# A seventeenth score tile per head group for VectorE, and a quarter of most images for GpSimd, in a one-core attention and spectral kernel

## The chip, the cores and the metric

One core of a Trainium2 chip. Its engines run side by side, each through its own list of instructions in order: TensorE (PE: matmuls, results in the banks of PSUM), ScalarE (ACT), VectorE (DVE), GpSimd (POOL, which works on SBUF here) and SyncE (SP, which issues DMAs). They wait for each other through semaphores. The metric is the device time of one execution in microseconds; lower is better.

## The reference, cut to what matters

```python
x = A_x                                       # 1 x 2048 x 512, bf16
x = x + _A_ref(_layernorm(x), A_w_r, A_w_i)   # irfft2(rfft2(x) * (w_r + i w_i))
x = x + _B_ref(_layernorm(x), wq, wk, wv, wo) # attention
x = x + _A_ref(_layernorm(x), A_w_r, A_w_i)
x = x + _B_ref(_layernorm(x), wq, wk, wv, wo)

def _B_ref(x, wq, wk, wv, wo):                # 32 heads of 16; one k and one v for all heads
    q = (x @ wq).reshape(B, S, 32, 16).transpose(0, 2, 1, 3)
    k = x @ wk
    v = x @ wv
    p = softmax(einsum("bhqd,bkd->bhqk", q, k) * 16 ** -0.5)
    return einsum("bhqk,bkd->bhqd", p, v).transpose(0, 2, 1, 3).reshape(B, S, 512) @ wo
```

Nearly all of the time goes into the exponentials of the two attention layers: 32 x 2048 x 2048 of them in each.

## The kernel before, in words

An attention layer works through 32 **groups** (`NG`): 4 blocks of 512 queries, each with 8 groups of 4 heads. The 2048 keys are cut into 16 chunks `kc` of 128, so a group has 64 **score tiles** (128 keys x 512 queries, one of 16 chunks and 4 heads). A score tile is one matmul with 32 rows of contraction (`score`, line 601), and its exponentials then go into a matmul with the values (`pv_step`, line 713) that adds up in one PSUM bank `pv` for the whole group. The values carry a column of ones, so that the sum of the exponentials comes out in the same bank.

Two engines make the exponentials, in two ways:

- **ScalarE** takes 48 of the 64 tiles, three at a time: `act_step(n)` writes three score tiles into the three banks of a PSUM tile `sc` (two buffers) and takes one `Exp` over all 1536 columns into `e` (line 701).
- **VectorE** takes the other 16, those with `h == kc % 4`. For each, `dve_step(n)` has a score matmul written into the one PSUM bank `dv` (one buffer) and turns it into 16-bit integers, a scaled logarithm: the **conversion** `t_new <- dv` (line 725). Four of them, of four neighbouring chunks, make a batch `b` of 4 x 512 integers. From each batch VectorE makes four **images** (lines 729 to 732): half the integers plus one of four offsets `PH_OFF`, whose bits are then read as bf16. The four images, each multiplied with values of its own weight (`vaug[:, j]`), add up to the exponential. So every VectorE tile needs four value matmuls, a ScalarE tile one.

The order is written out by hand. The layer is a run of **steps** `n`, one for each `e`; a group has 16 of them (the first group 18). In a step come, in this order, work put off by earlier steps (`todo`), the eviction of the group before, `dve_step`, `act_step`, `pv_step`. `chain()` ties each engine's instructions into exactly this order. In every step of a steady group VectorE does one conversion and one image, 16 and 16 per group. Value matmuls come two steps after their exponentials (`LAG = 2`).

The change of group lies in the third and fourth step of the next group:

```python
o, den = evict(evict_at[n])          # step 2: o <- pv, PSUM to SBUF, VectorE (line 616)
...
qproj(qproj_at[n], ps)               # step 2: queries of a later group, four matmuls into the freed pv bank
later(1, lambda ...: QT.__setitem__(g, qevict(ps)))   # step 3: qt <- ps and a bitwise and, VectorE (lines 464, 465)
```

In step 6 VectorE takes the reciprocal of the sums (line 624), which SP's DMAs bring and spread again. From step 12 on GpSimd multiplies `o` with them in three cuts (`product`, line 657). `pace` (line 605) makes such a GpSimd instruction wait for the latest image that VectorE has been given, so that it begins when that image has ended.

Around the two attention layers lie the spectral layers (Fourier transforms as matmuls), whose work the change does not touch. Their tile `U` (tag `G` of the pool `shared`) is free while attention runs.

Of the kernel before, what the change touches and what calls it, by code (L numbers as in the profile page):

```python
# [10 lines left out]
ALU = mybir.AluOpType  # L11
P = 128
BF = mybir.dt.bfloat16
F32 = mybir.dt.float32
I32 = mybir.dt.int32
S, D, H, DH = 2048, 512, 32, 16
NF = D // 2 + 1
NT = 16
NC = 4
R = 4  # L20
T = 4
# [5 lines left out]
I16 = mybir.dt.int16  # L27
# [15 lines left out]
def host_tables():  # L43
    import ml_dtypes
    bf = lambda a: np.ascontiguousarray(np.asarray(a, dtype=np.float32).astype(ml_dtypes.bfloat16))
    f32 = lambda a: np.ascontiguousarray(np.asarray(a, dtype=np.float32))
    w0 = 2 * np.pi / 2048.0
    tabs = {}

    sp = (128 * np.arange(4)[None, None, :, None] + np.arange(P)[:, None, None, None]).astype(np.float64)  # L50
    tt = np.arange(4)[None, :, None, None].astype(np.float64)
    k1 = np.arange(256)[None, None, None, :].astype(np.float64)
    ang = w0 * k1 * (4 * sp + tt)
    alt = np.broadcast_to(1.0 - 2.0 * (sp % 2), ang.shape[:3] + (1,))
    tabs["FT"] = bf(np.concatenate([np.cos(ang), -np.sin(ang)[..., 1:], alt], axis=3))

    s1 = np.arange(512)[None, None, None, :].astype(np.float64)
    kk = (128 * np.arange(2)[None, None, :, None] + np.arange(P)[:, None, None, None]).astype(np.float64)
    angi = w0 * kk * (4 * s1 + tt)
    wgt = np.where(kk == 0, 0.5, 1.0)  # L60
    it = np.stack([wgt * np.cos(angi), -np.sin(angi)], axis=2)
    it[0, :, 1, 0, :] = 1.0 - 2.0 * (np.arange(512) % 2)
    tabs["IT"] = bf(it)

    dd = (128 * np.arange(4)[None, :, None] + np.arange(P)[:, None, None]).astype(np.float64)
    ff = (np.arange(256)[None, None, :] + 1).astype(np.float64)
    angd = 2 * np.pi * dd * ff / 512.0
    tabs["DT"] = bf(np.stack([np.cos(angd), np.sin(angd), -np.sin(angd), 2 * np.sin(angd), -2 * np.sin(angd)], axis=2))
    fr = (128 * np.arange(2)[None, :, None] + np.arange(P)[:, None, None] + 1).astype(np.float64)
    d1 = np.arange(512)[None, None, :].astype(np.float64)  # L70
    angp = 2 * np.pi * fr * d1 / 512.0
    cfac = np.where(fr == 256, 1.0, 2.0) / (S * D)
    tabs["PS"] = bf(np.stack([cfac * np.cos(angp), cfac * np.sin(angp), -cfac * np.sin(angp)], axis=2))

    col = np.arange(64)
    c_, k2_, q_ = col // 32, (col // 8) % 4, col % 8
    base = 32 * k2_ + 8 * c_ + q_
    sel = np.zeros((P, 5, 64))
    sel[base, 0, col] = 1.0
    sel[(128 - base) % 128, 1, col] = 1.0  # L80
    sel[127 - base, 2, col] = 1.0
    sel[:, 3:5] = -sel[:, 1:3]
    tabs["SEL"] = bf(sel)
    selx = np.zeros((P, 2, 4))
    for i, (p_, sg) in enumerate(((16, 1), (48, 1), (112, -1), (80, -1))):
        selx[p_, 0, i] = 1.0
        selx[p_, 1, i] = sg
    tabs["SELX"] = bf(selx)
    eye = np.eye(P, dtype=np.float32)
    half = (np.arange(P) % 32) // 16  # L90
    tabs["KAB"] = f32(np.stack([1.0 - half, -THETA * half], axis=1))
    tabs["QAND"] = np.ascontiguousarray(np.broadcast_to(np.where(half == 0, -1, 0x7FFF).astype(np.int16)[:, None], (P, 512)))
    tabs["ident"] = bf(eye)
    return tabs

# [350 lines left out]
def attention_inputs(nc, tabs, shared, xn_sb, aw):  # L446
# [15 lines left out]
    def qevict(ps):  # L462
        qt = shared.tile([P, 512], BF, tag="QT", bufs=3)
        nc.vector.tensor_copy(out=qt, in_=ps)  # L464
        nc.vector.tensor_tensor(out=qt.bitcast(I16), in0=qt.bitcast(I16), in1=tabs["QAND"], op=ALU.bitwise_and)  # L465
        return qt

    def filler(psum, rhs, n):
# [60 lines left out]
def attention_layer(nc, tc, tabs, shared, lnpool, x_sb, xn_sb, aw, prep, nxt, store):  # L529
    with ExitStack() as ctx:  # L530
# [24 lines left out]
        NG = NQB * HG  # L555
        s0 = {}
        act_tiles = []
        for g in range(NG):
            s0[g] = len(act_tiles)
            us = [(g, kc, h) for kc in range(NT) for h in range(4)  # L560
                  if h != kc % 4 or (g == 0 and kc < 4)]
            act_tiles += [us[i:i + 3] for i in range(0, len(us), 3)]
        s0[NG] = len(act_tiles)
        d_score, d_phase = {}, {}
        for g in range(NG):
            for kc in range(NT):
                if not (g == 0 and kc < 4):
                    d_score[s0[g] + kc - 4] = (g, kc)
                    if g == 0:
                        base = 4 + (kc // 4 - 1) * 4  # L570
                    else:
                        base = s0[g] + kc - kc % 4
                    d_phase[base + kc % 4] = (g, kc // 4, kc % 4)
        LAG = 2
        first_pv, last_pv = {}, {}
        pv_list = {}
        evict_at = {s0[g + 1] + LAG: g for g in range(NG)}
        qproj_at = {s0[g + 1] + LAG: g + 2 for g in range(NG - 2)}
        for n0 in range(s0[NG]):
            lst = []  # L580
            if n0 in d_phase:
                g, b, j = d_phase[n0]
                lst += [(g, 4 * b + i, i, j, n0) for i in range(4)]
            lst += [(g, kc, h, -1, n0) for (g, kc, h) in act_tiles[n0]]
            assert len({u[0] for u in lst}) == 1
            n = n0 + LAG
            if n in evict_at:
                n += 1
            pv_list.setdefault(n, []).extend(lst)
            for u in lst:  # L590
                first_pv.setdefault((u[0], u[2]), u)
                last_pv[(u[0], u[2])] = u

        psc = ctx.enter_context(tc.tile_pool(name="psc", bufs=2, space=bass.MemoryType.PSUM))
        psd = ctx.enter_context(tc.tile_pool(name="psd", bufs=1, space=bass.MemoryType.PSUM))
# [3 lines left out]
        def score(dst, g, kc, h):  # L599
            hs = slice(32 * h, 32 * h + 32)  # L600
            nc.tensor.matmul(dst, lhsT=KT[hs, kc * P:(kc + 1) * P], rhs=QT[g][hs, :], start=True, stop=True)  # L601
# [3 lines left out]
        def pace(ins):  # L605
            if image[0] is not None:
                tc.add_manual_dep(ins.ins, image[0].ins.name, mybir.DependencyInfo(
                    mybir.DependencyClass.Sync, mybir.DependencyReason.DATA), reason="pace")
# [80 lines left out]
                store(r, t, nc.sync if t == T - 1 and r % 2 == 1 else nc.gpsimd)  # L689

        chain()
        def act_step(n):
            if n >= s0[NG]:
                return
            sc = psc.tile([P, 3, 512], F32, tag="sc")
            for i, (g, kc, h) in enumerate(act_tiles[n]):
                score(sc[:, i, :], g, kc, h)
            na = len(act_tiles[n])
            e = work.tile([P, 3, 512], BF, tag="e", bufs=7)
            ex[n] = e  # L700
            nc.scalar.activation(out=e[:, 0:na, :], in_=sc[:, 0:na, :], func=ACT.Exp, scale=SCALE)  # L701

        def pv_step(n):
            for u in pv_list.get(n, ()):
                g, kc, h, j, n0 = u
                if g not in pv:
                    pv_new = psp.tile([P, 512], F32, tag="pv")
                    pv[g] = pv_new
                if j < 0:
                    rhs = ex[n0][:, act_tiles[n0].index((g, kc, h)), :]  # L710
                else:
                    rhs = sb[(g, kc // 4, j)][:, h, :].bitcast(BF)
                nc.tensor.matmul(pv[g][32 * h:32 * h + 32, :], lhsT=vaug[:, max(j, 0), kc, :], rhs=rhs,  # L713
                                 start=(g > 0 and first_pv[(g, h)] == u), stop=(last_pv[(g, h)] == u),
                                 skip_group_check=True)

        def dve_step(n):
            if n in d_score:
                g, kc = d_score[n]
                dv = psd.tile([P, 512], F32, tag="dv")  # L720
                score(dv, g, kc, kc % 4)
                if kc % 4 == 0:
                    t_new = work.tile([P, 4, 512], I16, tag="T", bufs=3)
                    tb[(g, kc // 4)] = t_new
                nc.vector.tensor_scalar(out=tb[(g, kc // 4)][:, kc % 4, :], in0=dv, scalar1=T_MUL, scalar2=T_ADD,  # L725
                                        op0=ALU.mult, op1=ALU.add)
            if n in d_phase:
                g, b, j = d_phase[n]
                s_new = work.tile([P, 4, 512], I16, tag="S", bufs=7)
                sb[(g, b, j)] = s_new  # L730
                image[0] = nc.vector.tensor_scalar(out=s_new, in0=tb[(g, b)], scalar1=0.5, scalar2=16384.0 + PH_OFF[j],  # L731
                                                   op0=ALU.mult, op1=ALU.add)

        for n in range(s0[NG]):
            now[0] = n
# [281 lines left out]
```

## Time and profile before

| | us |
|---|---|
| median of 3 runs | 1649.36 (1648.85 to 1650.64) |
| the profiled execution's own time | 1655.24 |
| span in its profile, first to last instruction | 1653.4 |
| PE, DVE, ACT, POOL busy | 1428.4, 1551.4, 1509.0, 163.2 |
| ACT, all `e` (1028) | 1387.5 |
| DVE, conversions (1016) and images (1016) | 695.5 and 698.6 |
| POOL, `product` in three cuts (186) | 104.4 |

A "busy" time is the union of the instructions' spans. VectorE's instructions overlap their neighbours: the next one is shown to start about 85 ns before the last one ends, so a mean of 0.69 us for a conversion stands for some 0.60 us of the engine's time. The profiled execution is 0.36% longer than the median of the runs; differences that are worked out from its rows are added to the median as they are. From the eviction of one group to that of the next the trace shows 21.6 us all through both attention layers.

### The profile page before, as it was taken

The numbers are of one execution on the slowest core, as the hardware profiler recorded it, in microseconds if no ns is written. First come the engines' busy times: TensorE is split into PE (matmuls) and PEld (weight loads), VectorE is DVE, ScalarE is ACT, GpSimd is POOL, SyncE is SP. The second block draws the span as 40 slices with busy tenths as digits, with TensorE's granted clock in tenths as the row PEclk, the third lists the DMA queues.
The fourth block names the chain that finished last, engine by engine and source line by source line (L and its number), as shares of the span: only waits on it lengthen the run. The fifth ranks groups of instructions, "written<-read, shape, count | busy, mean of one in ns | idle before, by whom it ended". The sixth has DMA issues, their size and how long they took to land.

```text
span 1653.4 us, 32260 instructions
## 1 busy us (share of the span) xinstructions
PE 1428.4 (86%) x12768; PEld 461.3 (28%) x12768; DVE 1551.4 (94%) x2793; ACT 1509.0 (91%) x1254; POOL 163.2 (10%) x277
## 2 busy tenths in 40 slices
PE   6798888888888888888988988888888888888887
PEld 2342222222222222222333322222222222222222
DVE  6979999999999999999778799999999999999995
ACT  5369999999999999999853799999999999999994
POOL 3210000000000000000102000000000000000002
PEclk9899999999999999999998999999999999999999
DMA  8000000000000010001020000000000000000002
GB/s 289 5 1 8 17 17 17 17 16 11 16 17 17 16 30 16 16 17 30 23 71 0 1 9 16 17 17 17 17 17 17 17 17 17 12 15 17 16 17 66
DMA packets 46536, 40.78 MB, mean 25 GB/s; under 512 B 30832, under 2 KB 34416, under 8 KB 46000
## 3 DMA queue, kind: packets, MB, share of 16 engines
q1 hardware_dynamic: 45712, 36.88, 7.9%
q8 instruction: 100, 1.64, 0.4%
q0 software_dynamic: 672, 1.84, 0.3%
q14 instruction: 52, 0.43, 0.1%
HBM read 33.57 MB, written 3.15 MB: 22 GB/s over the span
## 4 chain that ended last, share of the span: by engine, by line
ACT 32%; DVE 29%; issue 21%; PE 16%; POOL 1%; DMA 1%; SPq 0%; DVEq 0%; POOLq 0%; ACTq 0%
ACT e L701 31%; DVE t_new L725 11%; DVE s_new L731 9%; PE pv_new L713 4%; PE fd L268 2%; PE dv L601 2%; DVE o L616 2%; DVE qt L464 2%; PE sc L601 2%; DVE qt L465 1%; DVE stats L125 1%; PE tri L679 1%; PE ps L391 1%; PE ps L379 1%; PE ps L192 1%
## 5 line engine op out<-in xcount | busy, mean ns | idle before, releaser
L701 ACT ACTIVATE e<-sc 128x1536 bf16<-128x1536 f32 (+1 forms) x1028 | 1387.5, 1532 | 6.2 <-PE sc L601 5.8
L725 DVE TENSOR_SCALAR t_new<-dv 128x512 int16<-128x512 f32 x1016 | 695.5, 685 | 26.4 <-PE dv L601 8.9
L731 DVE TENSOR_SCALAR s_new<-t_new 128x2048 int16<-128x2048 int16 x1016 | 698.6, 689 | 0.0
L601 PE MATMUL dv<-qt,KT 32*128 32x512 bf16 x1016 | 384.1, 378 | 108.1 <-DVE t_new L725 106.0
L601 PE MATMUL sc<-qt,KT 32*128 32x512 bf16 x3080 | 409.0, 383 | 33.9 <-ACT e L701 4.3
L713 PE MATMUL pv_new<-s_new,vaug 128*32 128x512 bf16 x4064 | 410.4, 391 | 27.2 <-DVE qt L464 27.2
L713 PE MATMUL pv_new<-e,vaug 128*32 128x512 bf16 x3080 | 412.9, 390 | 0.3 <-ACT e L701 0.3
L601 PEld LDWEIGHTS <-KT 32*128 32x128 bf16 x4096 | 201.2, 91 | 721.4 <-issue 702.8
L713 PEld LDWEIGHTS <-vaug 128*32 128x32 bf16 x7144 | 135.3, 94 | 265.7 <-issue 251.2
L657 POOL TENSOR_TENSOR ot_new<-o,rb 128x176 bf16<-128x176 f32 (+1 forms) x96 | 55.0, 575 | 700.0 <-DVE s_new L731 649.3
L657 POOL TENSOR_TENSOR od<-o,rb 128x176 bf16<-128x176 f32 (+1 forms) x90 | 49.4, 549 | 598.7 <-DVE s_new L731 598.7
L459 PE MATMUL ps<-xT,wq_sb 128*128 128x512 bf16 x256 | 67.3, 387 | 11.4 <-DVE o L616 11.4
L379 PE MATMUL ps<-tab_PS,st 128*128 128x512 bf16 x128 | 36.1, 448 | 16.2 <-DVE st L327 12.7
L385 ACT CAST U<-ps 128x512 bf16<-128x512 f32 x24 | 14.0, 585 | 36.4 <-PE ps L379 36.4
L268 PE MATMUL fd<-X,tab_DT 128*128 128x512 bf16 x192 | 43.9, 390 | 2.7 <-DVE X L242 2.7
L274 ACT CAST xn_sb<-fd 128x512 bf16<-128x512 f32 x32 | 18.7, 585 | 28.5 <-PE fd L268 28.5
L464 DVE CAST qt<-ps 128x512 bf16<-128x512 f32 x64 | 44.2, 691 | 0.4 <-PE ps L459 0.4
L616 DVE COPY o<-pv_new 128x512 f32<-128x512 f32 x64 | 43.8, 685 | 0.2 <-PE dv L601 0.2
L125 DVE BATCH_NORM_STATS2 stats<-x_sb 128x6 f32<-128x512 bf16 x46 | 30.7, 676 | 7.2 <-DMA x_sb<-in_A_x_dram 3.5
L459 PEld LDWEIGHTS <-wq_sb 128*128 128x128 bf16 x256 | 25.0, 97 | 40.2 <-issue 16.6
L391 PE MATMUL ps<-U,IT 128*128 128x512 bf16 x128 | 34.3, 390 | 0.0
L192 PE MATMUL ps<-FT,xn_sb 128*128 128x512 bf16 x80 | 22.2, 439 | 13.9 <-ACT xn_sb L134 10.9
(154 smaller groups left out, 602.1 us busy)
## 6 DMA issues: line engine op xcount, KB each, us to landing
rb<-d SPq DMA_DIRECT2D x256, 64.0 KB
FT<-const_FT SPq DMA_DIRECT2D x8, 512.0 KB
IT<-const_IT SPq DMA_DIRECT2D x8, 512.0 KB
x_sb<-in_A_x_dram SPq DMA_DIRECT2D x4, 512.0 KB
ot_new<-od SPq DMA_DIRECT2D x120, 16.0 KB
out_dram<-x_sb POOLq DMA_DIRECT2D x14, 128.0 KB, 2.2
tab_DT<-const_DT SPq DMA_DIRECT2D x1, 1280.0 KB
wr_raw<-in_A_w_r_dram SPq DMA_DIRECT2D x1, 1028.0 KB
```

The costliest lines, as they stand in the source:

```text
L268: nc.tensor.matmul(pss[i], lhsT=DT[:, b, w, 128 * fb:128 * fb + 128], rhs=X[:, b, part, c, :, :].rearrange("p k j -> p (k j)"), start=star ...
L379: nc.tensor.matmul(ps, lhsT=st[c][:, t, vec, q, fb, :], rhs=PS[:, fb, w, :], start=(k == 0), stop=(k == 3))
L391: nc.tensor.matmul(ps, lhsT=IT[:, t, part, c, r * P:(r + 1) * P], rhs=U[:, t, part, c, :], start=(k == 0), stop=(k == 3 and r % 2 == 1), s ...
L459: nc.tensor.matmul(ps, lhsT=wq_sb[:, c, hg, :], rhs=xTq[qb][:, c, :], start=(c == 0), stop=(c == NC - 1))
L464: nc.vector.tensor_copy(out=qt, in_=ps)
L601: nc.tensor.matmul(dst, lhsT=KT[hs, kc * P:(kc + 1) * P], rhs=QT[g][hs, :], start=True, stop=True)
L616: nc.vector.tensor_copy(out=o, in_=pv.pop(g))
L657: pace(nc.gpsimd.tensor_tensor(out=dst[:, a:b], in0=o[:, a:b], in1=rb[:, a:b], op=ALU.mult))
L701: nc.scalar.activation(out=e[:, 0:na, :], in_=sc[:, 0:na, :], func=ACT.Exp, scale=SCALE)
L713: nc.tensor.matmul(pv[g][32 * h:32 * h + 32, :], lhsT=vaug[:, max(j, 0), kc, :], rhs=rhs, start=(g > 0 and first_pv[(g, h)] == u), stop=(l ...
L725: nc.vector.tensor_scalar(out=tb[(g, kc // 4)][:, kc % 4, :], in0=dv, scalar1=T_MUL, scalar2=T_ADD, op0=ALU.mult, op1=ALU.add)
L731: image[0] = nc.vector.tensor_scalar(out=s_new, in0=tb[(g, b)], scalar1=0.5, scalar2=16384.0 + PH_OFF[j], op0=ALU.mult, op1=ALU.add)
```

## The change

For all groups but the first of a layer:

- The score tile of chunk 11 and head 0 (`EXTRA`) leaves ScalarE. In step 11 `sc` still gets three score tiles, but `Exp` covers two of them (1024 columns), and VectorE reads the third bank itself, with a second conversion in that step (`to_steps`). So VectorE has 17 tiles and ScalarE 47.
- The seventeenth tile becomes the fifth part of batch 3, whose four images are now 5 x 512 wide.
- Of the batches 0 to 2, VectorE makes three images and GpSimd the fourth, in four instructions of 512 columns, one per step, each behind `pace`.
- The 13 images that VectorE keeps are spread anew over the 16 steps: batch 0's in steps 0, 1 and 4, batch 1's in 5 to 7, batch 2's in 8 to 10, batch 3's in 12 to 15. Steps 2, 3 and 11 have none.
- Value matmuls go through a queue, at most three entries a step, emptied ahead of each eviction; there are 115 in place of 112 per group.
- The integers of all batches lie in one tile `scratch` in the place of `U`, three slots in turn; images have six buffers instead of seven, GpSimd's two of their own.
- `QAND` is one column, and the bitwise and of `qt` a `tensor_scalar` with it in place of a `tensor_tensor` with a full table.

In the first group GpSimd makes the fourth images of batches 1 and 2; it has no seventeenth tile.

```diff
-        nc.vector.tensor_tensor(out=qt.bitcast(I16), in0=qt.bitcast(I16), in1=tabs["QAND"], op=ALU.bitwise_and)
+        nc.vector.tensor_scalar(out=qt.bitcast(I16), in0=qt.bitcast(I16), scalar1=tabs["QAND"], scalar2=None, op0=ALU.bitwise_and)
...
+        EXTRA = (11, 0)
...
+                act_tiles += [[(g, kc, h) for h in range(4) if h != kc % 4 and (kc, h) != EXTRA] for kc in range(NT)]
...
+                for i in range(4):
+                    d_score[s0[g] + 4 * b + i - 4] = (g, b, i)
+                at = s0[g] + 4 * b
+                if b == 3:
+                    steps = (0, 1, 2, 3)
+                    if g > 0:
+                        batch[(g, b)].append(EXTRA)
+                        d_extra[s0[g] + EXTRA[0]] = (g, b)
+                else:
+                    steps = ((0, 1, 4), (1, 2, 3), (0, 1, 2))[b]
+                    for i in range(4):
+                        p_image[at + i] = (g, b, i)
+                for j, k in enumerate(steps):
+                    d_image[at + k] = (g, b, j)
...
+            count = len(queue) if n + 1 in evict_at else min(len(queue), 3)
...
+        scratch = shared.tile([P, 3, 5, 512], I16, tag="G", bufs=1)
...
+        def to_steps(g, b, i, ps):
+            nc.vector.tensor_scalar(out=steps_of(g, b)[:, i, :], in0=ps, scalar1=T_MUL, scalar2=T_ADD,
+                                    op0=ALU.mult, op1=ALU.add)
+
         def act_step(n):
...
+            if n in d_extra:
+                score(sc[:, 2, :], d_extra[n][0], *EXTRA)
             e = work.tile([P, 3, 512], BF, tag="e", bufs=7)
             ex[n] = e
             nc.scalar.activation(out=e[:, 0:na, :], in_=sc[:, 0:na, :], func=ACT.Exp, scale=SCALE)
+            if n in d_extra:
+                to_steps(*d_extra[n], 4, sc[:, 2, :])
...
+            if n in d_image:
+                g, b, j = d_image[n]
+                s_new = work.tile([P, 5, 512], I16, tag="S", bufs=6)
                 sb[(g, b, j)] = s_new
-                image[0] = nc.vector.tensor_scalar(out=s_new, in0=tb[(g, b)], scalar1=0.5, scalar2=16384.0 + PH_OFF[j],
-                                                   op0=ALU.mult, op1=ALU.add)
+                k = len(batch[(g, b)])
+                image[0] = nc.vector.tensor_scalar(out=s_new[:, 0:k, :], in0=tb[(g, b)][:, 0:k, :], **image_of(j))
+            if n in p_image:
+                g, b, i = p_image[n]
+                if i == 0:
+                    pool_new = work.tile([P, 4, 512], I16, tag="SP", bufs=2)
+                    sb[(g, b, 3)] = pool_new
+                pace(nc.gpsimd.tensor_scalar(out=sb[(g, b, 3)][:, i, :], in0=tb[(g, b)][:, i, :], **image_of(3)))
```

More of the change, by code (lines that the diff above doesn't have):

```diff
@@ L91, in host_tables @@
     tabs["KAB"] = f32(np.stack([1.0 - half, -THETA * half], axis=1))
-    tabs["QAND"] = np.ascontiguousarray(np.broadcast_to(np.where(half == 0, -1, 0x7FFF).astype(np.int16)[:, None], (P, 512)))
+    tabs["QAND"] = np.ascontiguousarray(np.where(half == 0, -1, 0x7FFF).astype(np.int16)[:, None])
     tabs["ident"] = bf(eye)
@@ L557, in attention_layer @@
         act_tiles = []
+        EXTRA = (11, 0)
         for g in range(NG):
             s0[g] = len(act_tiles)
-            us = [(g, kc, h) for kc in range(NT) for h in range(4)
-                  if h != kc % 4 or (g == 0 and kc < 4)]
-            act_tiles += [us[i:i + 3] for i in range(0, len(us), 3)]
+            if g == 0:
+                us = [(g, kc, h) for kc in range(NT) for h in range(4) if h != kc % 4 or kc < 4]
+                act_tiles += [us[i:i + 3] for i in range(0, len(us), 3)]
+            else:
+                act_tiles += [[(g, kc, h) for h in range(4) if h != kc % 4 and (kc, h) != EXTRA] for kc in range(NT)]
@@ L563, in attention_layer @@
         s0[NG] = len(act_tiles)
-        d_score, d_phase = {}, {}
+        d_score, d_extra, d_image, p_image, batch = {}, {}, {}, {}, {}
         for g in range(NG):
[L566 to L573, printed above, removed]
+            for b in range(NT // 4):
+                if g == 0 and b == 0:
+                    continue
+                batch[(g, b)] = [(4 * b + i, i) for i in range(4)]
+                for i in range(4):
[6 more added lines that the diff above has]
+                        d_extra[s0[g] + EXTRA[0]] = (g, b)
+                else:
+                    steps = ((0, 1, 4), (1, 2, 3), (0, 1, 2))[b]
[3 more added lines that the diff above has]
+                    d_image[at + k] = (g, b, j)
@@ L574, in attention_layer @@
         LAG = 2
-        first_pv, last_pv = {}, {}
-        pv_list = {}
+        first_pv, last_pv, pv_list = {}, {}, {}
         evict_at = {s0[g + 1] + LAG: g for g in range(NG)}
         qproj_at = {s0[g + 1] + LAG: g + 2 for g in range(NG - 2)}
[L579 to L586, printed above, removed]
-            if n in evict_at:
-                n += 1
-            pv_list.setdefault(n, []).extend(lst)
-            for u in lst:
+        queue = []
@@ new lines, in attention_layer @@
+        for n in range(s0[NG] + LAG):
+            n0 = n - LAG
+            if n0 in d_image:
+                g, b, j = d_image[n0]
+                queue.append([(g, kc, h, j, i) for i, (kc, h) in enumerate(batch[(g, b)])])
+            if n0 in p_image and p_image[n0][2] == 3:
+                g, b, _ = p_image[n0]
+                queue.append([(g, kc, h, 3, i) for i, (kc, h) in enumerate(batch[(g, b)])])
+            if 0 <= n0:
+                queue.append([(g, kc, h, -1, (n0, i)) for i, (g, kc, h) in enumerate(act_tiles[n0])])
+            if n in evict_at:
+                continue
+            count = len(queue) if n + 1 in evict_at else min(len(queue), 3)
+            pv_list[n] = sum(queue[:count], [])
+            queue = queue[count:]
+            for u in pv_list[n]:
@@ L591, in attention_layer @@
                 first_pv.setdefault((u[0], u[2]), u)
                 last_pv[(u[0], u[2])] = u
+            assert len({u[0] for u in pv_list[n]}) <= 1
+        assert not queue
         psc = ctx.enter_context(tc.tile_pool(name="psc", bufs=2, space=bass.MemoryType.PSUM))
@@ L691, in attention_layer, with steps_of @@
         chain()
+        scratch = shared.tile([P, 3, 5, 512], I16, tag="G", bufs=1)
+        def steps_of(g, b):
+            k = len(tb)
+            if (g, b) not in tb:
+                tb[(g, b)] = scratch[:, k % 3]
+            return tb[(g, b)]
+        def to_steps(g, b, i, ps):
+            nc.vector.tensor_scalar(out=steps_of(g, b)[:, i, :], in0=ps, scalar1=T_MUL, scalar2=T_ADD,
+                                    op0=ALU.mult, op1=ALU.add)
         def act_step(n):
@@ L701, in act_step @@
             nc.scalar.activation(out=e[:, 0:na, :], in_=sc[:, 0:na, :], func=ACT.Exp, scale=SCALE)
+            if n in d_extra:
+                to_steps(*d_extra[n], 4, sc[:, 2, :])
         def pv_step(n):
             for u in pv_list.get(n, ()):
-                g, kc, h, j, n0 = u
+                g, kc, h, j, k = u
                 if g not in pv:
@@ L709, in pv_step @@
                 if j < 0:
-                    rhs = ex[n0][:, act_tiles[n0].index((g, kc, h)), :]
+                    rhs = ex[k[0]][:, k[1], :]
                 else:
-                    rhs = sb[(g, kc // 4, j)][:, h, :].bitcast(BF)
+                    b = 3 if k == 4 else kc // 4
+                    rhs = sb[(g, b, j)][:, k, :].bitcast(BF)
                 nc.tensor.matmul(pv[g][32 * h:32 * h + 32, :], lhsT=vaug[:, max(j, 0), kc, :], rhs=rhs,
@@ L715, in pv_step, with image_of @@
                                  skip_group_check=True)
+        def image_of(j):
+            return {"scalar1": 0.5, "scalar2": 16384.0 + PH_OFF[j], "op0": ALU.mult, "op1": ALU.add}
         def dve_step(n):
             if n in d_score:
-                g, kc = d_score[n]
+                g, b, i = d_score[n]
                 dv = psd.tile([P, 512], F32, tag="dv")
[L721 to L725, printed above, removed]
-                                        op0=ALU.mult, op1=ALU.add)
-            if n in d_phase:
-                g, b, j = d_phase[n]
-                s_new = work.tile([P, 4, 512], I16, tag="S", bufs=7)
-                sb[(g, b, j)] = s_new
-                image[0] = nc.vector.tensor_scalar(out=s_new, in0=tb[(g, b)], scalar1=0.5, scalar2=16384.0 + PH_OFF[j],
-                                                   op0=ALU.mult, op1=ALU.add)
+                score(dv, g, 4 * b + i, i)
+                to_steps(g, b, i, dv)
+            if n in d_image:
+                g, b, j = d_image[n]
+                s_new = work.tile([P, 5, 512], I16, tag="S", bufs=6)
+                sb[(g, b, j)] = s_new
+                k = len(batch[(g, b)])
[6 more added lines that the diff above has]
+                pace(nc.gpsimd.tensor_scalar(out=sb[(g, b, 3)][:, i, :], in0=tb[(g, b)][:, i, :], **image_of(3)))
         for n in range(s0[NG]):
```

## The prediction

> **What bounds the kernel now.** I read the busy times first, then one group by the windows view, then the groups of instructions, then VectorE's and TensorE's timelines.
>
> ```profile
> PE 1428.4 (86%) x12768; PEld 461.3 (28%) x12768; DVE 1551.4 (94%) x2793; ACT 1509.0 (91%) x1254; POOL 163.2 (10%) x277
> ...
> L701 ACT ACTIVATE e<-sc 128x1536 bf16<-128x1536 f32 (+1 forms) x1028 | 1387.5, 1532 | 6.2 <-PE sc L601 5.8
> L725 DVE TENSOR_SCALAR t_new<-dv 128x512 int16<-128x512 f32 x1016 | 695.5, 685 | 26.4 <-PE dv L601 8.9
> ```
>
> The page: two engines are nearly full. The `Exp` row idles 6.2 us in all of 1387.5.
>
> ```profile
> 469.00:490.60 21.60, 18.75 (x181) 5.66 (x180) 21.38 (x37) 21.60 (x18) 1.65 (x3) 0.95 0.06 18
> ```
>
> One group in the windows view (PE, PEld, DVE, ACT, POOL busy, granted clock): ScalarE has no gap in 21.60 us, VectorE 0.2. ScalarE sets the period: 16 `e` of 1386.5 / 1026 = 1.351 us (the rows kept apart by form). VectorE catches up after each change of group; there it runs at its own pace:
>
> ```profile
> 510.38 0.68 DVE L731 TENSOR_SCALAR s_new<-t_new 128x2048 int16<-128x2048 int16 x1
> 511.12 0.69 DVE L725 TENSOR_SCALAR t_new<-dv 128x512 int16<-128x512 f32 x1
> 511.72 0.68 DVE L731 TENSOR_SCALAR s_new<-t_new 128x2048 int16<-128x2048 int16 x1
> 512.32 0.69 DVE L616 COPY o<-pv_new 128x512 f32<-128x512 f32 x1
> 512.92 0.68 DVE L725 TENSOR_SCALAR t_new<-dv 128x512 int16<-128x512 f32 x1
> 513.52 0.69 DVE L731 TENSOR_SCALAR s_new<-t_new 128x2048 int16<-128x2048 int16 x1
> 514.15 0.69 DVE L464 CAST qt<-ps 128x512 bf16<-128x512 f32 x1
> 514.87 0.43 DVE L465 TENSOR_TENSOR qt<-qt,tab_QAND 128x512 int16<-128x512 int16 x1
> 515.22 0.69 DVE L725 TENSOR_SCALAR t_new<-dv 128x512 int16<-128x512 f32 x1
> ```
>
> Start to start, a conversion, an image or `o` takes 0.60; `qt` 0.72, the and 0.35. `qt` starts 1.83 after `o`, since `qproj` (513.06 to 514.11 in TensorE's timeline) needs `o` done; the conversion and the image between them hide that.
>
> ```profile
> 499.72 0.69 DVE L725 TENSOR_SCALAR t_new<-dv 128x512 int16<-128x512 f32 x1
> ...
> 500.46 0.37 PE L601 MATMUL dv<-qt,KT 32*128 32x512 bf16 x1 [0.25 <-DVE t_new L725]
> ...
> 500.92 0.69 DVE L725 TENSOR_SCALAR t_new<-dv 128x512 int16<-128x512 f32 x1
> ```
>
> The whole timeline: `dv` is one bank. A conversion ends (500.41), then the next score is made (500.46 to 500.83), then comes the next conversion: never under 1.20 from one to the next out of `dv`. The image between them hides that too.
>
> The last reading is GpSimd beside the images:
>
> ```profile
> 504.74 0.56 POOL L657 TENSOR_TENSOR ot_new<-o,rb 128x176 bf16<-128x176 f32 x1 [18.67 <-DVE s_new L731]
> ```
> ```profile
> 505.12 0.73 DVE L731 TENSOR_SCALAR s_new<-t_new 128x2048 int16<-128x2048 int16 x1
> 505.77 0.68 DVE L725 TENSOR_SCALAR t_new<-dv 128x512 int16<-128x512 f32 x1
> ```
>
> The product ends at 505.30, the image at 505.85. In all images of the trace that last over 0.70, the end lies 0.55 behind a product's end; a product that ends within the first 0.13 of an image leaves it at 0.68. So an image does not run while GpSimd works: it ends 0.55 after GpSimd at the earliest. Conversions, which read PSUM, stay at 0.68 beside products. `pace` keeps today's products (0.52 to 0.57) within one conversion.
>
> **The change, part by part**, for a steady group (image n is that of step n; from image end to image end).
>
> *ScalarE.* `e` of step 11 loses 512 columns. Two 512-wide ones take 1387.5 - 1386.5 = 1.0, so 0.50 each; (1.351 - 0.50) / 2 = 0.43 off: ScalarE's sum falls from 21.60 to 21.17. That is all that can be won while ScalarE is the bound.
>
> *VectorE's plain sum.* 17 conversions and 9 images at 0.60 (15.6); four images of 2560 columns (the two `KT` rows of line 480, 404 for 512 and 674 for 1536 columns, give 0.135 per 512 more: 0.735, 2.94); `o` 0.60, `qt` 0.72, the and as `tensor_scalar` (0.404 by the 512-wide `KT` row against 0.426: 0.33), the reciprocal 0.16: 20.35. Were there no waits, ScalarE would stay the bound. There are four.
>
> *GpSimd's images against VectorE's.* The trace has no 16-bit integer instruction on GpSimd. The nearest row in kind and size is line 136 (`tensor_scalar`, 512 columns of bf16, two scalars): 0.768 in 22, 0.75 start to start; the bounds are the 160-wide product (0.52) and the 512-wide one of two inputs (line 651, 1.26). I take 0.768, the row of one input; by 1.26 the seven stretches below would each be 0.49 longer, 213 us in all, which I give 0.02. Products start 0.08 after the image that they wait for. From image to image a step with GpSimd's image between takes 0.08 + 0.77 + 0.55 = 1.40, in place of 1.20. Seven stretches are such: 0 to 1 and 4 to 10 (six). The Trainium skill ("SBUF — State Buffer", Who interferes with whom) says that a VectorE operation in a two-port mode and a GpSimd operation exclude each other and that the second one "fully blocks". The trace agrees that they exclude each other but has 0.55 behind the product, not an image's whole 0.685; by the whole one a stretch would be 1.53.
>
> *Image 1 to image 4.* `o` starts 0.085 before image 1 ends. Without an image in step 2, VectorE waits for `qproj`: `qt` 1.83 after `o`, then 0.72 and 0.33 to the conversion of step 3. The conversion of step 4 follows it with nothing between, so 1.20 later (one `dv` bank); image 4 starts 0.60 after and lasts 0.685. Sum: -0.085 + 1.83 + 0.72 + 0.33 + 1.20 + 0.60 + 0.685 = 5.28. GpSimd's images of steps 1 to 3 run back to back to 0.08 + 3 x 0.75 + 0.02 = 2.35, just ahead of the and (2.47). The two images taken out save little here: they covered these two waits.
>
> *Image 10 to image 12.* In the changed program's order, listed with its waits, the second conversion of step 11 waits not for its score but for `e` of the same step, which reads the same tile; the conversion and the image of step 12 are queued behind it. The scores of step 11 are made when the conversion of step 10 has freed `dv`, so `e` starts some 0.21 before the conversion of step 11, lasts 1.53 - 0.43 = 1.10, and the second conversion starts 0.94 after the first in place of 0.60. (Bounds: no wait, or one more `e`, 1.35, if ScalarE lags by a buffer; after image 4 it is starved, so it shouldn't.) Then 0.60 and 0.60 and an image of 0.82: -0.085 + 0.94 + 1.20 + 0.82 = 2.88. GpSimd's last two images and the first cut of the product are done at 2.16, and 2.16 + 0.55 + 0.135 = 2.85 is no later.
>
> *The rest.* 12 to 15: 3 x 1.335 = 4.00 (a cut's 0.08 + 0.56 + 0.55 + 0.135 = 1.33 fits). 15 to 0: 1.20. The reciprocal fits into a 1.40.
>
> Sum: 1.40 + 5.28 + 6 x 1.40 + 2.88 + 4.00 + 1.20 = 23.16. ScalarE's 21.17 is under that, so VectorE becomes the bound and loses 23.16 - 21.60 = 1.56 per group. With 62 groups: 97 us.
>
> *At no cost.* Three more value matmuls: a round of up to four takes 0.22, TensorE's step goes to four rounds, some 1.1, under 1.20; were that cover gone, 3 x 0.22 x 62 = 41 us. `scratch` slots wait for GpSimd's images of four or more steps before; the wait would show in conversions. SP's transfer of `od` and the release of `o` sit behind GpSimd's images; products still start in step 12, as before. The first groups keep 18 steps, ScalarE bound. The smaller `QAND` load ends long before its use.
>
> Total: 1649.36 + 97 = 1746 for the median, 1655.24 + 97 = 1752 for a profiled execution.
>
> **The rivals.**
>
> *Short images on GpSimd* (0.57 or less, like the products): the seven stretches are 1.20, the reciprocal shows: 23.16 - 1.40 + 0.16 = 21.92, +0.32 x 62 = 20: 1669. For: the products; against: 22 rows of 0.768. In the Trainium skill, "GPSIMD Engine Reference", Engine selection calls one-input work roughly line-rate; line 136's row does not agree (0.768, where VectorE's own line 804 has 0.41).
>
> *Long images* (0.91, as line 804's 0.908, the same form beside VectorE's `tensor_scalar`): seven stretches +0.14 (0.98), the and +0.2, image 12 +0.25: 1.43 more: 1746 + 89 = 1835.
>
> *Whole blocking* by the page's words: 7 x 0.135 = 0.95 more, 1805. Against: every blocked image ends 0.55 after.
>
> *ScalarE stays the bound*, the faster side: the plain sum holds, and the time is 1649 - 0.43 x 62 = 1623. It decides once VectorE's chain is under 21.17, 2.0 below my sum: GpSimd's images would have to hide wholly (1.40), the wait for `e` be nil (0.34), and a part of the 1.15 in steps 2 to 4 go (0.55 before `qt`, 0.60 before step 4). For: VectorE's plain 20.35. Against: the three rows above.
>
> *No difference*: the gain of the third bank and the waits cancel, 1649.
>
> **How the numbers follow.** Forecast 0.57 (own range 1715 to 1780, from a wait for `e` of 0 to 0.6 and an image on GpSimd of 0.70 to 0.83), short images 0.14, long ones 0.16 (0.02 of it by 1.26), whole blocking 0.04, ScalarE 0.06, no difference 0.03. A measurement of this kernel tells 0.2% (3.3 us) from no change. Faster 0.06, same 0.03, slower 0.91. The range goes from short to long images, 1665 to 1838; it leaves out about 0.1, since without either end it would hold too little.
>
> **What would show it.** In the changed profile: groups 23.2 apart; ScalarE's `e` waiting for scores (idle of some 2 us per group); GpSimd's images at 0.77 and VectorE's stretches 4 to 10 at 1.40, their images shown longer than 0.69; a gap of 0.5 before `qt` and before the conversion of step 4; 0.3 before the second conversion of step 11, ended by `e`. I am wrong if ScalarE has no gaps, or if images beside GpSimd's stay at 0.69.

## The result: slower, and the profile after

The changed kernel takes 1752.07 us (1748.78 to 1755.17), the kernel before 1649.46: 1.0621 times as long, with an interval of 1.0600 to 1.0642. Forecast were 1746 and a range of 1665 to 1838. The profiled execution has a span of 1753.4. Evictions lie 23.39 apart on average (60 groups away from the ends of the layers; before 21.62), with 22.96 as the shortest and most frequent distance. Of 60 x 1.77 = 106 us the two spans show 100. The last groups of the two layers are 1.6 shorter in all than before, and the parts ahead of, between and behind the two runs of evictions take 303 in place of 308. That part is no gain of the change: the profiled execution of the kernel before had a granted clock of 0.95 there, and the kernel without the seventeenth tile (below), at 1.00, takes 303 as well.

First the page, with its rows for ScalarE, GpSimd's new images and the second conversion of step 11:

```profile
PE 1338.2 (76%) x12954; PEld 464.7 (27%) x12954; DVE 1530.4 (87%) x2665; ACT 1504.2 (86%) x1254; POOL 622.2 (35%) x1037
...
L736 ACT ACTIVATE e<-sc 128x1536 bf16<-128x1536 f32 (+2 forms) x1028 | 1383.0, 1445 | 115.3 <-PE sc L622 110.5
L775 POOL TENSOR_SCALAR pool_new<-scratch 128x512 int16<-128x512 int16 x760 | 463.5, 619 | 784.5 <-DVE s_new L769 703.5
...
L722 DVE TENSOR_SCALAR scratch<-sc 128x512 int16<-128x512 f32 x62 | 42.9, 692 | 62.1 <-ACT e L736 62.1
```

No engine is nearly full any more. `Exp` idles 115 us, 110 of it for scores (before 6), and the 62 second conversions wait 62 us for `Exp`: ScalarE and VectorE wait for each other in turn. GpSimd's images take 0.62, not 0.77.

One group in the windows view (PE, PEld, DVE, ACT, POOL, granted clock):

```profile
474.06:497.03 22.97, 16.65 (x183) 5.73 (x183) 20.95 (x36) 21.47 (x17) 8.90 (x15) 1.00 0.05 14
```

VectorE and ScalarE both have gaps now, 2.0 and 1.5. VectorE's timeline of this group shows where:

```profile
474.06 0.67 DVE L637 COPY o<-pv_new 128x512 f32<-128x512 f32 x1
474.66 0.68 DVE L722 TENSOR_SCALAR scratch<-dv 128x512 int16<-128x512 f32 x1
475.85 0.69 DVE L464 CAST qt<-ps 128x512 bf16<-128x512 f32 x1 [0.52 <-PE ps L459]
...
477.99 0.69 DVE L722 TENSOR_SCALAR scratch<-dv 128x512 int16<-128x512 f32 x1 [0.46 <-PE sc L622]
...
482.42 0.73 DVE L769 TENSOR_SCALAR s_new<-scratch 128x2048 int16<-128x2048 int16 x1
...
486.88 0.67 DVE L722 TENSOR_SCALAR scratch<-dv 128x512 int16<-128x512 f32 x1
488.56 0.69 DVE L722 TENSOR_SCALAR scratch<-sc 128x512 int16<-128x512 f32 x1 [1.01 <-ACT e L736]
```

ScalarE's timeline of the same group (neighbours merged) and one line of GpSimd's:

```profile
476.28 1.45 ACT L736 ACTIVATE e<-sc 128x1536 bf16<-128x1536 f32 x1 [0.57 <-PE sc L622]
478.10 11.77 ACT L736 ACTIVATE e<-sc 128x1536 bf16<-128x1536 f32 x9 [0.38 <-PE sc L622]
490.42 8.16 ACT L736 ACTIVATE e<-sc 128x1536 bf16<-128x1536 f32 x6 [0.55 <-PE sc L622]
```
```profile
481.98 0.62 POOL L775 TENSOR_SCALAR pool_new<-scratch 128x512 int16<-128x512 int16 x1 [0.68 <-DVE s_new L769]
```

The three together give the period. In steps 2 to 4 VectorE waits for `qproj` (0.52) and for the `dv` bank (0.46; the profile names the scores of `sc`, which TensorE makes right behind that of `dv`). TensorE's scores are late with it, and ScalarE starves (0.57, 0.38). From 478.10 on ScalarE runs without a gap to the `Exp` of step 11, 1.33 from start to start. VectorE's images end 1.24 to 1.32 apart in that stretch, so it arrives early and waits 1.01 until that `Exp` has ended. Then ScalarE starves again (0.55), since the conversion of step 12 was queued behind the wait. So from `o` to step 4 the time is that of the chain through `qproj`, `qt` and the `dv` bank, from there to step 11 ScalarE's, and from the second conversion to the next `o` VectorE's.

### The profile page after: what moved, and what is told of

It reads as the page before. It is cut to its first block, busy times and chain, and to the rows that moved or that the text cites. A ratio compares the mean times of both kernels' runs of the same rounds, so it can differ in the third digit from the quotient of the medians.

```text
span 1753.4 us, 34139 instructions
## 1 busy us (share of the span) xinstructions
PE 1338.2 (76%) x12954; PEld 464.7 (27%) x12954; DVE 1530.4 (87%) x2665; ACT 1504.2 (86%) x1254; POOL 622.2 (35%) x1037
## 4 chain that ended last, share of the span: by engine, by line
DVE 48%; PE 24%; ACT 13%; issue 12%; DMA 1%; POOL 1%; SPq 0%; POOLq 0%; ACTq 0%; DVEq 0%
DVE scratch L722 24%; DVE s_new L769 14%; ACT e L736 11%; PE pv_new L751 7%; PE dv L622 7%; PE ps L459 4%; DVE o L637 2%; DVE qt L464 2%; PE fd L268 2%; DVE stats L125 1%; PE ps L391 1%; PE sc L622 1%; PE ps L192 1%; PE ps L379 1%; DVE den L645 1%
## 5 line engine op out<-in xcount | busy, mean ns | idle before, releaser
L736 ACT ACTIVATE e<-sc 128x1536 bf16<-128x1536 f32 (+2 forms) x1028 | 1383.0, 1445 | 115.3 <-PE sc L622 110.5
L775 POOL TENSOR_SCALAR pool_new<-scratch 128x512 int16<-128x512 int16 x760 | 463.5, 619 | 784.5 <-DVE s_new L769 703.5
L722 DVE TENSOR_SCALAR scratch<-dv 128x512 int16<-128x512 f32 x1016 | 688.0, 677 | 61.5 <-PE sc L622 50.2
L769 DVE TENSOR_SCALAR s_new<-scratch 128x2048 int16<-128x2048 int16 x826 | 628.1, 761 | 0.1
L751 PE MATMUL pv_new<-e,vaug 128*32 128x512 bf16 x3018 | 450.8, 397 | 0.0
L622 PE MATMUL sc<-qt,KT 32*128 32x512 bf16 x3080 | 424.3, 400 | 3.3 <-DVE scratch L722 1.4
L751 PEld LDWEIGHTS <-vaug 128*32 128x32 bf16 x7330 | 155.8, 95 | 307.7 <-issue 277.4
L722 DVE TENSOR_SCALAR scratch<-sc 128x512 int16<-128x512 f32 x62 | 42.9, 692 | 62.1 <-ACT e L736 62.1
L751 PE MATMUL pv_new<-pool_new,vaug 128*32 128x512 bf16 x760 | 75.6, 388 | 0.0
L136 POOL TENSOR_SCALAR xn_sb<-x_sb,rstd,nb 128x512 bf16<-128x512 bf16 x22 | 16.8, 767 | 86.4 <-DVE nb L131 76.4
```

Source lines behind the costliest of these rows:

```text
L722: nc.vector.tensor_scalar(out=steps_of(g, b)[:, i, :], in0=ps, scalar1=T_MUL, scalar2=T_ADD, op0=ALU.mult, op1=ALU.add)
L769: image[0] = nc.vector.tensor_scalar(out=s_new[:, 0:k, :], in0=tb[(g, b)][:, 0:k, :], **image_of(j))
L775: pace(nc.gpsimd.tensor_scalar(out=sb[(g, b, 3)][:, i, :], in0=tb[(g, b)][:, i, :], **image_of(3)))
```

## Experiments

The kernels vary the changed one; the edits stand in the changed kernel's lines. "Theory G" in the expectations is the prediction's own first term, "theory W" the reading above.

**The second conversion ahead of `Exp`.**

```diff
             if n in d_extra:
                 score(sc[:, 2, :], d_extra[n][0], *EXTRA)
+                to_steps(*d_extra[n], 4, sc[:, 2, :])
...
             nc.scalar.activation(out=e[:, 0:na, :], in_=sc[:, 0:na, :], func=ACT.Exp, scale=SCALE)
-            if n in d_extra:
-                to_steps(*d_extra[n], 4, sc[:, 2, :])
```

> The second conversion of step 11 is put ahead of that step's Exp, so that Exp waits for the conversion and not the conversion for Exp. Theory W (the wait for Exp is on the path that sets the period, and it hides the shorter stretches 4 to 10): the conversion starts 0.6 after the first one instead of 1.66, image 12 ends 1.1 earlier after `o` (15.4 instead of 16.5), groups some 22.0 apart: 1670 to 1690. Theory G (GpSimd's exclusion of the images on the way from image 4 to image 10 is what costs): ScalarE is only held up longer, nothing gained, 1745 to 1755.

Measured: 1677.75, ratio to the kernel before 1.0169 (1.0150 to 1.0188), groups mostly 22.08 apart: 74 us less than the change. The wait has turned round, as ScalarE's rows, kept apart by form, show:

```profile
L737 ACT ACTIVATE e<-sc 128x1536 bf16<-128x1536 f32 x964 | 1309.8, 1481 | 15.4 <-PE sc L622 15.0
L737 ACT ACTIVATE e<-sc 128x1024 bf16<-128x1024 f32 x62 | 63.5, 1024 | 39.4 <-DVE scratch L722 39.4
```

The 1024-wide `Exp` now idles 39.4 / 62 = 0.64 for VectorE. The waits for scores fell from 110.5 to 15.0. Theory W holds. Not all of the 74 us is the wait itself: some 24 are TensorE's clock, as worked out at the end of the account of the prediction.

**GpSimd's images left out.** The diff drops the `if n in p_image` branch, and in `pv_step`:

```diff
-                    rhs = sb[(g, b, j)][:, k, :].bitcast(BF)
+                    rhs = sb[(g, b, (1 if b == 0 else 2) if j == 3 and b < 3 else j)][:, k, :].bitcast(BF)
```

> GpSimd's images are left out; their value matmuls read an image of VectorE's instead, so this part of the result is not computed. Theory W: image 0 to image 1 is 0.13 shorter, but the second conversion of step 11 still waits for Exp, whose chain from step 4 on is as long as before: 22.8 per group, 1740 to 1750. Theory G: all seven stretches shorten on the path (image 4 to image 10 from 7.67 to 7.35, image 0 to 1 from 1.33 to 1.20): 0.45 to 0.6 per group, 1712 to 1725.

Measured: 1746.7, ratio 1.0582 (1.0563 to 1.0602), 5 us under the change. The images' row of the changed kernel, then VectorE's rows in this one:

```profile
L769 DVE TENSOR_SCALAR s_new<-scratch 128x2048 int16<-128x2048 int16 x578 | 424.7, 735 | 0.1
```
```profile
L769 DVE TENSOR_SCALAR s_new<-scratch 128x2048 int16<-128x2048 int16 x578 | 394.2, 682 | 0.1
...
L722 DVE TENSOR_SCALAR scratch<-sc 128x512 int16<-128x512 f32 x62 | 42.9, 692 | 86.5 <-ACT e L736 86.5
```

The images are back at 0.68 (0.74 in the changed kernel). They save 30 us, and most of that VectorE waits longer for `Exp`: 86.5 in place of 62.1. The clock blurs the comparison of the times, since this execution has 53 stretches at half clock and the changed kernel's has 40. Groups without such a stretch are 22.84 apart here and 22.99 there on average, so the exclusion by GpSimd costs 0.15 per group, some 9 us. It is real and, in this kernel, mostly hidden behind the wait. Theory G, which has 0.45 at the least, falls; theory W has 22.8.

**The seventeenth tile back to ScalarE**, the rest of the change kept:

```diff
-                act_tiles += [[(g, kc, h) for h in range(4) if h != kc % 4 and (kc, h) != EXTRA] for kc in range(NT)]
+                act_tiles += [[(g, kc, h) for h in range(4) if h != kc % 4] for kc in range(NT)]
...
-                    if g > 0:
-                        batch[(g, b)].append(EXTRA)
-                        d_extra[s0[g] + EXTRA[0]] = (g, b)
```

> The seventeenth tile goes back to ScalarE: 48 and 16, images of batch 3 are 2048 wide again; GpSimd's images and the steps without image stay. Theory W: with the wait for Exp gone, ScalarE's 21.6 and VectorE's chain are about level: 1645 to 1670. Theory G, by the terms of the prediction (image 10 to 12 then 2.4, three images 0.135 shorter, the rest unchanged: 22.3 per group): 1685 to 1700.

Measured: 1649.09, ratio 0.9990 (0.9979 to 1.0000), 21.55 per group. ScalarE's row:

```profile
L733 ACT ACTIVATE e<-sc 128x1536 bf16<-128x1536 f32 (+1 forms) x1028 | 1385.1, 1525 | 7.2 <-PE sc L619 6.7
```

Without this tile nothing is lost. ScalarE idles 7.2 us in all, so it covers GpSimd's images and the steps without image.

**An image in step 3 in place of step 1.**

```diff
-                    steps = ((0, 1, 4), (1, 2, 3), (0, 1, 2))[b]
+                    steps = ((0, 3, 4), (1, 2, 3), (0, 1, 2))[b]
```

> Batch 0's second image is made in step 3 instead of step 1 (images in 0, 3, 4): it fills the 0.55 us in which VectorE waits for the dv bank before the conversion of step 4, and step 1 has the copy of `o` behind its conversion. Theory: image 4 ends 5.2 to 5.3 after `o` as before, but `o` comes 0.7 earlier: 22.2 to 22.3 per group, 1705 to 1715. Rival (the value matmuls of the group before, not VectorE, release `o`): no gain, 1745 to 1755.

Measured: 1711.54, ratio 1.0376 (1.0351 to 1.0400), 22.38 at the least: 41 us less. The conversions' waits for scores, 50.2 us in the changed kernel, are nearly gone:

```profile
DVE scratch L722 <- PE sc L622: 12.4, 21, 1.2
```

The gap before the conversion of step 4 was on the path. At full clock it cost 22.96 - 22.38 = 0.58 per group, close to the 0.60 that the prediction gave it.

**Both edits that made it faster**: the conversion ahead of `Exp` (first diff) and the image in step 3 (the diff above).

> Both together: the second conversion of step 11 ahead of Exp, and images of batch 0 in steps 0, 3, 4. Theory: the two savings add on VectorE's chain (22.08 - 0.70 = 21.4 per group), and ScalarE, whose plain sum is 21.17, is close behind: 21.3 to 21.5, a little under the 21.6 of the kernel before: 1632 to 1645. Rival (Exp, which now waits for VectorE, costs ScalarE 0.65 per group wherever it lies: 21.17 + 0.65 = 21.8): 1655 to 1668.

Measured: 1670.03, ratio 1.0131 (1.0115 to 1.0146), 21.93 per group. The theory misses. The 62 `Exp` of 1024 columns idle 43.7 us for VectorE, 0.70 each, and ScalarE's 21.17 + 0.70 = 21.87 is nearly the whole period: the rival's mechanism, at a price a little over its own, so that the time lies 2 us above the rival's range.

**The seventeenth tile in step 2**, its conversion behind that step's `Exp`. (Slots of `scratch` go by `(4 * g + b) % 3`, so that the earlier first touch leaves them as they were.)

```diff
-        EXTRA = (11, 0)
+        EXTRA = (2, 0)
```

> The seventeenth tile is that of chunk 2 and head 0 and so its conversion lies in step 2, behind that step's Exp as in the change: VectorE waits there for qproj anyway. Step 11 has neither an image nor a second conversion. Theory W: Exp of step 2 ends some 1.3 after `o`, the conversion delays `qt` by 0.1 to 0.2 only, and step 12's conversion waits 0.6 for the dv bank: 22.0 to 22.1 per group, 1668 to 1684. Rival (the wait for Exp costs about 1 us wherever it lies): 1735 to 1755.

Measured: 1725.17, ratio 1.0462 (1.0447 to 1.0478), mostly 22.7 per group. Neither was right. I took over where `Exp` of step 2 stands in the changed kernel, 0.18 behind the start of `o`. With the gap of step 11 gone it starts 0.79 behind it, the conversion starts 2.0 after `o`, `qt` 2.6 after it in place of 1.8, and all that hangs on `qt` is 0.8 later.

**No seventeenth tile, and the image in step 3**: the diffs of those two experiments together.

> No seventeenth tile, and images of batch 0 in steps 0, 3, 4. Theory: without the tile ScalarE's 16 Exp over 1536 columns (21.55) set the period, so what VectorE saves brings nothing: 1645 to 1651. Rival (VectorE's chain sets it there too): 0.5 to 0.7 less per group, 1605 to 1620.

Measured: 1642.27, ratio 0.9959 (0.9944 to 0.9974): 0.4% faster than the kernel before, 21.49 per group. The theory, that nothing is gained, misses by 3 us. ScalarE's timeline shows what bounds it, one line for more than a group:

```profile
424.95 23.30 ACT L733 ACTIVATE e<-sc 128x1536 bf16<-128x1536 f32 x17
```

No gap: the first of the 17 is shown with 1.81, and each of the others ends 1.343 after the one ahead of it. 16 x 1.343 = 21.49 is the period, so ScalarE is full, as the theory has it. In the kernel before an `Exp` ends 1.343 to 1.344 after the one ahead of it too, at a granted clock of 0.95, so the clock does not make the difference. But one `Exp` of each group, that of step 4, ends 1.444 after the one ahead: it starts at 516.47, 0.11 after its scores are done. This 0.10 per group, some 6 us in all, is what the order here takes away. The rows show no idle time for it, because the spans of neighbouring `Exp` overlap.

**The second conversion ahead of `Exp`, without GpSimd's images**: the first two diffs together.

> The second conversion of step 11 ahead of Exp, and GpSimd's images left out (their value matmuls read an image of VectorE's, so this part of the result is not computed). Theory: with the wait for Exp gone the stretches 4 to 10 lie on the path, and now the exclusion shows: image 4 to image 10 from 7.70 to 7.35, image 0 to 1 from 1.3 to 1.2, so 0.4 to 0.5 per group, or as much of it as ScalarE leaves: 1645 to 1658 against 1678 with them. Rival (the exclusion costs nothing there either): 1672 to 1680.

Measured: 1650.39, ratio 1.0012 (1.0002 to 1.0021), 21.63 per group, 27 us under the same kernel with them. Where the wait for `Exp` is gone the exclusion does show, 0.45 per group. The 1024-wide `Exp` still waits for the conversion, 0.25 each time:

```profile
ACT e L737 <- DVE scratch L722: 15.0, 60, 0.3
```

**The seventeenth tile in step 2, its conversion ahead of `Exp`** (the first diff and `EXTRA = (2, 0)`), with the image in step 3 and, next, without that:

> The seventeenth tile is that of chunk 2 and head 0; its conversion lies in step 2 ahead of that step's Exp, in the time in which VectorE waits for qproj and ScalarE is about to wait for scores; images of batch 0 in steps 0, 3, 4. Theory W (the second reader of the tile waits for the first, and the price is set by how long it idles there): the conversion hides before `qt` (still 1.8 after `o`), Exp of step 2 starts at 1.9 after `o`, and the next two follow with 0.1 to 0.2 lost: VectorE's chain 21.3, ScalarE 21.2: 1630 to 1642. Rival (Exp loses 0.7 to 0.9 there as in step 11): 21.8 to 22.0 per group, 1660 to 1672.

> As the run before, with the images of batch 0 left in steps 0, 1, 4. Theory W: VectorE's chain is longer by the gap before the conversion of step 4, 21.9 to 22.0 per group, and ScalarE has time to spare: 1665 to 1676. Rival (ScalarE sets the period in both): the same time as the run before.

Measured: 1655.41, ratio 1.0042 (1.0027 to 1.0057), 21.72 per group, and 1672.92, ratio 1.0144 (1.0128 to 1.0160), 21.94. The second is as theory W has it. The first lies between the two; VectorE's timeline and ScalarE's:

```profile
426.42 0.68 DVE L721 TENSOR_SCALAR scratch<-dv 128x512 int16<-128x512 f32 x1
427.01 0.68 DVE L721 TENSOR_SCALAR scratch<-sc 128x512 int16<-128x512 f32 x1
427.61 0.69 DVE L464 CAST qt<-ps 128x512 bf16<-128x512 f32 x1
```
```profile
427.79 3.71 ACT L736 ACTIVATE e<-sc 128x1024 bf16<-128x1024 f32 x3 [0.54 <-DVE scratch L721]
```

The conversion hides ahead of `qt` entirely, but `Exp` waits 0.54 for it and no starving follows that could make up for it: 21.17 + 0.54 = 21.71. In every place tried the tile read by two engines made one of them wait. With GpSimd's images this was 0.54 to 1.0 per group, more than the 0.43 that ScalarE gains; without them it was 1.4 behind `Exp` and 0.25 ahead of it, and the last of these lost next to nothing against the kernel before. A tile of its own for the third bank was not tried, so that it would end the wait is not shown.

## Why the prediction was right, and where its steps were not

**ScalarE's gain.** The 1024-wide `Exp` lasts 1.095; 1.10 was worked out. The 21.17 that it led to holds the 0.10 per group that ScalarE lost at the change of group in the kernel before; the prediction read that group as one without a gap.

**Image 1 to image 4.** 5.14 against 5.28: 0.52 for `qproj` and 0.46 for the `dv` bank. The experiment with the image in step 3 confirms the second with 0.58 per group.

**GpSimd's images against VectorE's.** The rule read from the products holds: GpSimd ends at 482.60, the image begun at 482.42 ends at 483.15, 0.55 behind. The Trainium skill ("SBUF — State Buffer", Who interferes with whom) says that the second of the two fully blocks. The trace agrees that they exclude each other, but not that the whole image comes behind: that would be 0.685. Why 0.135 of it is already done is not shown. The term itself was mis-sized: 0.62 per instruction, not the 0.768 of the bf16 row, so image 0 to 1 and image 4 to 10 take 1.33 + 7.67 = 9.00 in place of 9.80. And it was put on the path: 5 us came back without those instructions (0.15 per group at full clock), not the 62 x 0.45 = 28 that a place on the path would have given.

**Image 10 to image 12.** The wait was read from the order and is there, but the step "after image 4 it is starved, so it shouldn't" lag failed. With GpSimd's shorter images VectorE's steps are quicker than ScalarE's 1.33 from step 4 on, and `Exp` of step 11 starts 0.5 after the first conversion, not 0.21 ahead of it. The second conversion starts 1.68 after the first in place of 0.94, and 2.88 became 3.63. This was the wait that was mis-sized most: it delays the second conversion by 1.08 in place of 0.34.

**The sum.** 23.16 - 0.80 + 0.75 - 0.14 = 22.97, and 22.96 is measured for a group at full clock. Two errors of the same size and opposite sign have cancelled, and the clock, no term of the sum, added 0.43 per group on average; that 1752 lies 6 us from the forecast 1746 is luck. The direction and the places of the waits were forecast. The largest of the causes was not: by the experiments it is the wait on `Exp` (74 us when turned round), then the gap before step 4 (41 us), and these overlap (82 us together); GpSimd's images come far behind in this order. Of the signs that the prediction named, ScalarE's idle time (115.3 / 62 = 1.9 per group) and the two gaps of 0.5 came. GpSimd's 0.77, the stretches of 1.40 and the 0.3 ahead of the second conversion did not: they are 0.62, 1.24 to 1.32 and 1.01.

**TensorE's clock** was no term of the sum and makes the remaining 0.43 per group. The windows view with the granted clock, a slow group and stretches of 5 us:

```profile
450.38:474.06 23.68, 17.87 (x183) 5.71 (x183) 21.11 (x35) 21.58 (x17) 8.90 (x15) 0.93 0.06 16
...
467.00:472.00 5.00, 4.34 (x38) 1.15 (x36) 4.46 (x7) 4.40 (x4) 1.05 (x2) 0.66 0.05 12
490.00:495.00 5.00, 4.03 (x46) 1.26 (x44) 5.00 (x8) 4.58 (x4) 1.08 (x2) 1.00 0.00 0
```

The last line is the same place in a group of 22.97. In 35 of the 60 groups the clock falls to half, mostly for 3.4 us, nearly always behind the wait of step 11; score matmuls take 0.60 instead of 0.38, and the time from one conversion out of the `dv` bank to the next, which paces VectorE there, grows. Groups without such a stretch are 22.99 apart on average, those with one 23.68.

At the wait of step 11 TensorE stands idle for 1.3 us, since its next scores need the `dv` bank. The four kernels in which the second conversion waits for `Exp` all have a longest idle stretch of 1.25 to 1.3 in a group (median of the groups). Between the first and last evictions of the layers they have 36 (the change), 50 (without GpSimd's images), 23 (image in step 3) and 13 (tile in step 2) stretches at half clock. In the other eight kernels, the one before among them, this median is 0.45 to 0.49, and there are none or one. So about 60 x 0.40 = 24 of the 74 us is the clock, a consequence of the wait.

The Trainium skill ("TensorE: Matmul & The Clock Gate", The HAM clock gate) has the clock at half after an idle window of about 3.4 us. The trace agrees with the length, 3.413 in 34 of the changed kernel's 40 stretches, but not with the idle time: between those evictions no gap between two matmuls is longer than 1.5. What decides which group is hit stays open.

## What to carry to other kernels

Where two engines are both nearly full, moving a piece from one to the other pays only if it ties them no more closely: here a shared tile made its second reader wait for the first, in whichever order, and with GpSimd's images beside it that cost more than the piece brought. Instructions that seem to be spare load may cover waits; ahead of taking one out, ask what its neighbours wait for. And a sum that hits does not prove its terms: undoing the parts one by one showed that the term for GpSimd's images, 1.40 of the sum, lay almost wholly off the path.

## What the runs showed of the hardware

- A `tensor_scalar` of 512 columns on GpSimd took 0.619 from 16-bit integers to 16-bit integers with constants for its scalars, and 0.767 for bf16 with scalars from memory (line 136), in the same run.
- An image of 2048 columns on VectorE that GpSimd holds up ends 0.55 after GpSimd's instruction, whether that was a product or an image; a plain one takes 0.68.
- An `Exp` of 1536 columns ends 1.343 after the one ahead of it when ScalarE is full, at a granted clock of 0.95 and of 1.00 alike, and takes 1.45 when it starts from idle. The profile shows longer ones, up to 1.81, when they start early, so a row can show no idle time where 0.10 is lost.
- The granted clock fell to 0.5, mostly for 3.4 us at a time, in the four kernels whose TensorE has a gap of 1.25 to 1.3 in a group (median), and at most once between the evictions of the eight where this median is 0.45 to 0.49. TensorE's busy share of the span does not order the four: 36 stretches at 76%, 50 at 80%, 23 at 77%, 13 at 80%.
